# Batch 1's centred rows turned by transposing DMAs, with the start of the order made anew

## The chip, the cores and the metric

The kernel runs on one core of a Trainium2 chip. The metric is the device time of one execution in microseconds (us); the median of several runs is compared. TensorE (PE) multiplies matrices, VectorE (DVE), ScalarE (ACT) and GpSimd (POOL) work element by element, SyncE (SP) issues most DMAs. Each engine works through its own queue in order, and the queues wait for each other by semaphores.

## The reference, cut to what matters

```python
# x: 8 x 8 x 512 x 64, state: 8 x 8 x 32 x 64 (batch, head, rows, 64), float32
a  = softmax(scale * x @ state^T, over the 32 state rows);  xread = a @ state      # 512 rows
a2 = softmax(scale * state @ x^T, over the 512 rows of x);  sread = a2 @ x         # 32 rows
x2 = concatenate([xread, sread], rows), heads laid side by side                    # 8 x 544 x 512
X = np.fft.fft(x2, axis=1)
X = np.fft.fft(X, axis=2)
u = x2 + np.real(X)
un = (u - mean(u)) / sqrt(var(u) + 1e-6)                                           # per row
out = u + np.maximum(un @ w_ch1, 0.0) @ w_ch2                                      # 512 -> 2048 -> 512
```

## The kernel before

The batches run one after the other, and each goes through four parts:

- `attend(b)`: the rows `xin` (the bfloat16 copy of the loaded `xs`) and the state `stb` are turned into `xT` and `sT`; products `esp` give the scores, exponentials on ScalarE give `E`, `EE` and `ET`; the products `xrp`, `xfp` and `srp` read with them, and the result is scaled into `XR` and `XF`, rows in reverse and in forward order.
- `transform(b)`: the two-dimensional Fourier transform as products with tables of sines and cosines: `gp` over the columns (copied to `G`), `yp` over the rows. `U` is the sum of a block of rows with its transform; a row's mean and variance are `mv`. `centre` writes the centred rows `ub` (bfloat16), and `turn_u` turns a block of 128 x 512 of them into columns of `unT`. There are four blocks for each batch.
- `layer1(b)`: products `ph` of `unT` with `w1`, and a relu on ScalarE into `hT`.
- `layer2(b)`: products `po` of `hT` with `w2`, scaled by `rstd` and added to `U` on VectorE (`ot`). From batch 2 on this is a form with fewer products (`poA`, `poB`).

`turn_x`, `turn_state` and `turn_u` have two forms. In one, four TensorE transposes write a PSUM tile (`xTp`, `sTp`, `tp`) and a copy takes it to SBUF. In the other, one transposing DMA on SP's queue does the same from SBUF to SBUF. Which is used is set by batch: `x_by_dma, u_by_dma = 2, 2` means that the DMA is used from batch 2 on for both.

Nothing is issued where it is written. A `Recorder` keeps every engine call as a numbered group, and `play` issues the groups in the order of the list `ORDER`, so that each engine's queue is that list restricted to its own groups. Every instruction therefore has the line of the recorder's helper (L63), and the profile is read by tile names. `BANKS` says in the same way which of six PSUM banks each product tile uses, and which buffer an output tile uses. In the first 70 us the layers of batch 0 are interleaved with the attention and the transform of batch 1 and with the attention of batch 2.

Some names of that stretch: `warm` products only keep TensorE busy while data is loading; a `gate` operation reads one or a few elements of a tile so that what stands behind it on its engine, or what reads the gate, comes after that tile; the weights come as eight DMAs on POOL's queue, four for `w1` and four for `w2`; `load_state(1, 2)` loads the state of batch 1 on SP's queue. ScalarE's sine (for the tables `TS`, `TC`) and exponential need different tables, and each change between them is an ACT_TABLE_LOAD; an activation on `gate2` asks for the sine's ahead of the tables:

```python
    nc.scalar.activation(gate2[:, 1:2], gate2[:, 0:1], AF.Sin)
    state_ones(0, 2)
    state_blocks(0, 1)
    cast_x(0, nc.scalar.copy, 2, 3)
```

Of the kernel before, what the change touches and what calls it, by code (L numbers as in the profile page):

```python
# [49 lines left out]
class _Engine:  # L50
# [3 lines left out]
    def __getattr__(self, what):  # L54
# [14 lines left out]
        19 62 66 61 9-10 12 1 7 11 2 5 4 3 163 8 49 13 6 298 14 55 15 17 16 50 22 0 75-82 29 143 25 27 26 47 28 38 31 41 23  # L69
        144-145 40 39 32 146-147 30 20 46 21 42 48 148 43-45 149 18 24 34-35 33 37 36 72-74 83-118 130 119 329 120-121 123 122  # L70
        155 131 157 124 156 168 330 172 125 141 170 126 169 171 173 142 176 127-129 133-134 184 178 180 192 68 54 159 69-71 177
        185 193 59-60 58 67 64 316 63 65 187 189 186 135-137 188 138 194 196 195 197 139-140 153-154 216 174 331-332 175 206-210
        212 179 211 181 221 219 213 222 132 150-151 182 152 190 198-199 191 217 214 218 200 263 160 167 201-202 51 265 161
        203-204 267-268 165-166 205 299 162 56 261-262 300 158 264 304 266 297 307 303 302 301 57 228 232 229 220 225-227 224
        233 245 223 244 241 183 215 236-240 252-254 231 235 234 230 276-277 247-248 278-279 246 250-251 259 257 255 269 256 272
        249 242-243 258 271 274 284 270 273 317 312 310 309 319 315 314 313 311 318 280-283 285 290 292-293 291 294 275 286 288
        323 322 287 327 326 320 289 321 328 343 324 341 325 345 339 347 340 348 355 333 337 353 378 351 335 386 354 352 346 387
        361 360 342 338 344 385 379 362-365 367 308 260 366 368 52 296 358 382 381 398 356 390-391 380 383-384 521 392-393 396
        394 439 401 400 399 336 357 359 397 334 402-404 406 405 408 407 409 522 413-414 505 523-524 410 415 412 411 441 525 305
        371 370 369 373 422 374 419 375 426 424 420 423 53 526 421 417-418 459 457 349 376 455 453 461 476 465 388 463 473 469  # L80
        467 460 395 350 440 462 456 454 377 458 464 470 468 466 389 472 488 474 480 518 451 481 445-446 449 482 450 487 484 491
        442 492 447 485 496 475 477-478 443 448 495 500-501 506 429-430 428 427 452 591 493 486 479 483 529 536 497 516 498 489
        517 502 499 490 578 164 306 579 507 503 574 527 504 471 508 372 576 580 528 575 416 577 433 432 435 437 434 431 436 543
        582 512 532 519 530 494 583 514 444 520 531 550 533 539 537 589 509 540 538 560-563 510 555 544 556 545 511 438 546 549
        772 547 553 548 559 552 557 554 584 558 598 592 534 585-586 630 622 600 564 569 567 601 606 614 587-588 593 602-603 573
        568 572 570-571 607-608 596 595 597 594 609-610 621 611 613 612 616-617 625 618 627 626 620 619 604 541 624 632 637 599
        535 551 631 615 605 590 623 638 542 652 677 633 641 639 635 565 634 642 640 636 646 661 668 628 566 653 662 678 647 649
        671 654 648 655 670 663 669 664 684 689 685 690 680 682 650 644 659 672 629 683 658 681 667 651 688 693 645 673 660
        714-715 751 704 736-737 757 761 716-717 701 656 700 740 699 295 698 718 728 727 729 657 730 733 732 731 581 674-675
        694-695 679 767 762 782 708 774-775 768 922 745 744 705 771 742 769 741 746 743 738 752 739 754 756 706 763-764 758 755  # L90
        753 776-777 709 778 783 779-780 791 786 790 794-795 787 789 788 702-703 676 713 796 697 765 818 812 864 784 792 802 797
        804 816 814 871 759 808 719 820 766 813 865 819 793 803 785 798 815 805 817 760 809 821 830 823 711 725 720 710 825 726
        712 707 722 806 810 873 799 828 734 880 837 723 721 826 824 827 735 800 781 801 747-748 849 862 842 831 872 807 874 829
        881 836 835 846 850 838 840 839 841 811 863 845 843 852 870 724 773 770 851 750 844 866 858 856 875 911 832 893 877 884
        882 892 833 883 876 857 696 853 859 867 887-888 919 904 886 902 907 974 908 889-890 912 903 921 665-666 891 822 896 691
        847 895 848 899 898 897 900-901 692 686 643 687 954 932 914 878 909-910 920 894 955 928-929 934 968 834 960 957 959 925
        923-924 879 1102 941-942 970 980 996 963 917 976 905 1035 991 987 939 969 975 997 1046 981 933 906 1036 964 918 992 940
        930 913 931 935 943 916 915 937 944-948 938 971 965 949 966 986 950 977 988 967 953 952 951 978 984 993 1103 927 936 958
        973 926 962 961 956 1047 989 982 1007 985 994 979 990 983 1008 1048 1003 998 1012 1040 1009 1053 1022 1024 1058 1101
        1000 999 1001 1014 1005 1013 1004 1002 1041 1006 1054 1010 1025 1011 1060 1086 1061 1051 1067 1077-1078 1049 1062  # L100
        1015-1016 1063 1023 1059 1018 1027 1052 1064 1070 868 1071 1073-1074 1072 860 869 861 854 1075-1076 855 1079-1080 1050
        1087 1140 1017 1026 1031 1042 1280 1105 1104 1107 515 1134 1139 1137-1138 1106 1082 1037 1097-1098 1055 1119 1146 1084
        1236 1112 1069 1065 1056 1083 1099-1100 1066 1088 1038 1091 1113 1132 1108 1148 1094 1213 1166 1164 1110 1120 1019 1028
        1147 1237 1133 1114 1089-1090 1115-1116 1118 1117 1126 1122 1095 1081 1121 1124 1123 1141 1096 1143 1142 1130 1125 1111
        1144 1158 1205 1154 1092 1193 1162 1168 1127 1160 1149 1032 1085 1214 1165 1043 1109 1159 1167 1155 1206 1093 1194 1169
        1145 1131 1128 1161 1163 1174 1231 1207 1188 1219 1150 1175-1177 1151 1178 1057 1039 1136 1135 513 1179 1232 1220
        1181-1182 1180 1279 995 1020-1021 425 1029 1238-1239 1183 1172 1225 1156 1264 1191 1229 1226 1157 1192 1230 1185 1208
        1173 1171 1186 1189 1240 1184 1241 1190 1187 1243 1201 1196 1224 1197 1281-1282 1129 1068 1153 1200 1285 1195 1283-1284
        1209 1215 1255 1245 1256 1260 1227 1288 1257-1258 1244 1228 1247 1274 1261 1198 1030 1242 1044 1248 1250 1254 1249 1170
        1253 1199 1045 1033-1034 1275-1276 1221 1233 1335 1272 1277 1222 1289 1259 1265 1304 1273 1278 1308 1268 1305 1270  # L110
        1290-1291 1315 1252 1251 1267 1316 1292 1266 1234 1286 1321 1331 1297 1364 1343 1319 1327 1337 1376 1310 1407 1262 1293
        1269 1294 1296 1306 1295 1322 1312 1314 1332 1344 1299 1313 1300 1303 1301 1309 1342 1361 1302 1271 1202 1210 1287 1336
        1298 1320 1328 1216 1377 1365 1395 1408 1311 1338 1333 1325 1339 1359 1329 1340 1334 1326 1330 1317 1354 1402 1390 1360
        1318 1391 1403 1263 1398 1378 1435 1409-1410 1345 1357 1356 1355 1358 1379 1411 1399 1412 1348 1346-1347 1349 1367 1372
        1352 1368 1353 1307 1323 1235 1223 1386 1380 1366 1371 1413 1419 1421 1211-1212 1420 1217 1424-1425 1203-1204 1218 1341
        1423 1422 1369-1370 1392 1404 1426-1427 1416 1400 1362 1446-1447 1396 1384 1350 1428 1436 1429 1440 1393 1405 1363 1373
        1397 1351 1385 1401 1454-1455 1481 1491 1431 1441 1474 1461 1536 1450 1492 1482 1475 1462 1451 1439 1438 1418 1448-1449
        1456-1457 1468 1437 1458 1460 1459 1463 1476 1478 1464 1414-1415 1432 1445 1465-1466 1452 1512 1570 1499 1501 1489 1443
        1453 1477 1467 1444 1430 1497 1493 1469 1479 1537 1442 1513 1500 1490 1502 1498 1494 1472 1470 1473 1480 1516 1483 1507
        1495 1485 1524 1563 1519 1517-1518 1496 1520 1486 1508 1510 1509 1504 1511 1394 1406 1521 1505 1433 1538 1484 1527 1381  # L120
        1532 1525 1514 1564 1387 1528 1434 1515 1506 1523 1539 1522 1544 1554 1567 1558 1556 1550 1557 1540 1546 1471 1526 1531
# [50 lines left out]
def kernel(  # L172
# [8 lines left out]
    nc = Recorder(tc.nc)  # L181
# [304 lines left out]
    def stats_of(u, name, roots=None):  # L486
# [12 lines left out]
        else:  # L499
            roots.append(root)  # L500
        return mv, rstd

    first_roots = []


    x_by_dma, u_by_dma = 2, 2


    turned = {}

    def attend(b):
        g4, bq = b // 4, b % 4
# [1042 lines left out]
```

## Time and profile before

| | |
|---|---|
| runs | 288.75, 287.68, 288.82 us; median 288.75 |
| profiled execution | 287.47 us, of which the span of the profile is 285.7 us |
| granted TensorE clock | 0.997 |
| busy: TensorE, VectorE, ScalarE, GpSimd | 275.2 (96%), 210.6 (74%), 162.0 (57%), 92.5 us (32%) |
| ACT_TABLE_LOAD | 4, of 1.28 us each, at 1.90, 6.32, 11.58 and 19.53 us |
| first layer-1 product of batch 0, of batch 1 | 22.39 us, 54.00 us |
| copies `unT<-tp` on ScalarE | 6 in batches 0 and 1, 565 to 587 ns each |
| transposing DMAs `unT<-ub` on SP | 26, from 75.0 us on |

A row of the timeline has the start and the duration in us, the engine, the operation with its output and inputs, and how many instructions the row holds; in brackets stands how long the engine was idle before it, and what ended that. Matmuls overlap, so the pace of TensorE is read from one start to the next, not from the duration of one. Times are from the start of the span.

### The profile page before, as it was taken

To read this page: it belongs to the slowest core of one execution; us is meant where nothing else is said; L and a number is where in the kernel's file an instruction comes from. 1 tells how busy PE (TensorE), PEld (TensorE's weight loads), DVE (VectorE), ACT (ScalarE), POOL (GpSimd) and SP (SyncE) were. 2 spreads that over 40 slices of the span, in tenths; PEclk is the share of its full clock that TensorE was granted. 3 is DMA by queue.
4 is the path that set the end of the run, shared out by engine and by line. 5 is a ranking of instruction groups with operands and counts; after the bars stand their busy time and mean duration, and the time that the engine had idled before them with its cause. 6 is when DMAs were issued, how large, how long until landed. Compare 5 with 4: busy or idle time off the path is not lost.

```text
span 285.7 us, 6835 instructions
## 1 busy us (share of the span) xinstructions
PE 275.2 (96%) x2615; PEld 199.0 (70%) x2644; DVE 210.6 (74%) x554; ACT 162.0 (57%) x327; POOL 92.5 (32%) x227
## 2 busy tenths in 40 slices
PE   7899999999999999999999999999999999999993
PEld 6788985555655778567758777576577667686882
DVE  6877777468899988985798688959766578224892
ACT  7897656746936576368377564586566653254000
POOL 8392476670660033502712119006200028000000
PEclk9999999999999999999999999999999999999998
DMA  8999959966366346861379640413201520978366
GB/s 156 185 181 190 202 95 181 197 146 153 83 157 103 93 116 156 107 170 25 80 169 194 149 94 19 98 53 65 84 0 48 151 65 18 182 149 136 92 162 184
DMA packets 110972, 34.91 MB, mean 122 GB/s; under 512 B 101996, under 2 KB 106476, under 8 KB 110940
## 3 DMA queue, kind: packets, MB, share of 16 engines
q1 hardware_dynamic: 100220, 28.72, 47.5%
q0 software_dynamic: 4224, 4.19, 9.7%
q10 hardware_dynamic: 6496, 1.57, 2.6%
q8 instruction: 20, 0.33, 0.5%
q14 instruction: 12, 0.10, 0.1%
HBM read 22.41 MB, written 14.02 MB: 128 GB/s over the span
## 4 chain that ended last, share of the span: by engine, by line
PE 87%; DVE 7%; DMA 2%; issue 1%; ACT 1%; SPq 1%; DVEq 0%
PE ph L63 39%; PE poA L63 18%; PE poB L63 13%; PE gp L63 4%; PE po L63 3%; PE yp L63 2%; DVE U L63 2%; DMA xs<-in_x_dram 2%; PE esp L63 2%; PE eTp L63 1%; PE xrp L63 1%; DVE XR L63 1%; PE xfp L63 1%; DVE ot L63 1%; SPq L63 1%
## 5 line engine op out<-in xcount | busy, mean ns | idle before, releaser
L63 PE MATMUL ph<-unT,w 128*128 128x512 bf16 (+2 forms) x743 | 127.9, 315 | 1.4
L63 ACT ACTIVATE hT<-ph 128x512 bf16<-128x512 f32 x128 | 72.1, 596 | 76.6 <-PE ph L63 76.3
L63 PEld LDWEIGHTS <-w 128*128 128x128 bf16 x768 | 64.3, 98 | 42.5 <-issue 0.6
L63 PEld LDWEIGHTS <-hT 128*128 128x128 bf16 x632 | 60.4, 98 | 14.8 <-issue 0.3
L63 DVE SCALAR_TENSOR_TENSOR ot<-poA,rstd,U 128x256 f32<-128x256 f32 (+1 forms) x46 | 21.7, 475 | 16.5 <-PE poA L63 13.8
L63 POOL CAST xin<-xs 128x2048 bf16<-128x2048 f32 (+3 forms) x14 | 14.5, 1046 | 48.5 <-PE poA L63 20.3
L63 PE MATMUL poB<-w,hT 128*128 128x256 bf16 x224 | 28.2, 273 | 0.0
L63 POOL TENSOR_TENSOR rstd<-rstd,mhalf 128x1 f32<-128x1 f32 x34 | 20.3, 604 | 1.1
L63 POOL TENSOR_TENSOR rstd<-mv,epst 128x1 f32<-128x1 f32 x14 | 2.8, 211 | 42.9 <-DVE mv L63 42.9
L63 ACT CAST G<-gp 128x288 bf16<-128x288 f32 (+2 forms) x31 | 12.8, 477 | 5.6 <-PE gp L63 5.3
L63 ACT ACTIVATE ub<-U,S 128x512 bf16<-128x512 f32 (+1 forms) x22 | 15.1, 706 | 1.5 <-DVE U L63 1.3
L63 PE MATMUL po<-w,hT 128*128 128x512 bf16 x60 | 15.4, 379 | 0.2
L63 PE MATMUL poB<-TA,SA 128*128 128x256 bf16 x120 | 15.5, 273 | 0.1
L63 PE MATMUL poA<-TA,SB 128*128 128x256 bf16 x120 | 15.6, 273 | 0.0
L63 DVE SCALAR_TENSOR_TENSOR U<-yp,XF 128x2 f32<-128x2 f32 (+1 forms) x24 | 10.0, 419 | 7.5 <-PE yp L63 5.3
L63 DVE SCALAR_TENSOR_TENSOR ot<-poB,rstd,ot 128x256 f32<-128x256 f32 x30 | 14.2, 478 | 1.0 <-PE poB L63 0.8
L63 PE MATMUL poA<-TC,hT 128*128 128x256 bf16 (+1 forms) x120 | 14.5, 265 | 0.1
L63 POOL COPY XT<-XR 32x514 bf16<-32x514 bf16 x7 | 4.2, 605 | 31.8 <-DVE U L63 15.8
L63 PE MATMUL poA<-w,hT 128*128 128x256 bf16 x112 | 14.5, 273 | 0.0
L63 ACT ACTIVATE junk<-U,S 128x512 bf16<-128x512 f32 x20 | 14.3, 716 | 0.2
L63 PE MATMUL poA<-TB,hT 128*128 128x256 bf16 x112 | 14.3, 273 | 0.0
L63 DVE SCALAR_TENSOR_TENSOR ot<-poB,rstd,U 128x256 f32<-128x256 f32 x15 | 7.2, 478 | 9.0 <-PE poB L63 9.0
(197 smaller groups left out, 478.3 us busy)
## 6 DMA issues: line engine op xcount, KB each, us to landing
xs<-in_x_dram SPq DMA_DIRECT2D x22, 256.0 KB, 3.8
w<-in_moe_w_ch_dram POOLq DMA_DIRECT2D x8, 512.0 KB, 6.8
out_dram<-ot SPq DMA_DIRECT2D x15, 256.0 KB, 2.4
r_dram<-ot SPq DMA_DIRECT2D x14, 256.0 KB, 2.4
out_dram<-r_dram SPq DMA_DIRECT2D x14, 256.0 KB, 3.7
xs<-in_x_dram SPq DMA_DIRECT2D x8, 192.0 KB, 4.9
xs<-in_x_dram ACTq DMA_DIRECT2D x2, 256.0 KB, 4.7
l_dram<-ot SPq DMA_DIRECT2D x2, 256.0 KB, 2.0
```

The source lines that it names most:

```text
L63: self._rec.add(self._name, lambda: f(*args, **kw), key)
```

## The change

`u_by_dma` goes from 2 to 1. Batch 1's four `turn_u1` calls each become one transposing DMA on SP's queue instead of four TensorE transposes and one copy on ScalarE, and the recorder has 1744 groups instead of 1748. The order is made anew for the part in which batches 0 and 1 are worked on; the last 568 groups are the same (their numbers 4 lower). The strings in `BANKS` are made anew as well. TensorE's own order is the same as before from about 70 us on. Batch 1's state load, twelfth on SP before, follows straight behind batch 0's loads.

```diff
 ORDER = [i for p in """
-        19 62 66 61 9-10 12 1 7 11 2 5 4 3 163 8 49 13 6 298 14 55 15 17 16 50 22 0 75-82 29 143 25 27 26 47 28 38 31 41 23
-        144-145 40 39 32 146-147 30 20 46 21 42 48 148 43-45 149 18 24 34-35 33 37 36 72-74 83-118 130 119 329 120-121 123 122
...
+        19 58 4 11-12 10 298 9 7 1 14 2 8 13 6 16 3 17 15 55 54 5 50 22 21 25 0 38 20 143 23 29-30 144 26 145-146 27 147 40 39
+        41 28 42-43 46 44 148 31 149 32 150 45 75-82 18 34 24 37 72 36 33 35 83-109 130 110-123 131 155 157 124 156 168 172 125
...
-    x_by_dma, u_by_dma = 2, 2
+    x_by_dma, u_by_dma = 2, 1
...
-    turn_u1(0, 1, nc.scalar.copy)
+    turn_u1(0, 1)
...
-    turn_u1(0, 0, nc.scalar.copy)
+    turn_u1(0, 0)
...
-    turn_u1(1, 1, nc.scalar.copy)
+    turn_u1(1, 1)
...
-    turn_u1(1, 0, nc.scalar.copy)
+    turn_u1(1, 0)
```

What the new order moves on each engine's queue, by name:

- ScalarE: the first cast `stb<-gen` of batch 0's state stands ahead of the `gate2` activation; it was behind it.
- SP: batch 1's state load, as told; a piece of `load_x(3)` and the pieces of `load_x(2)` stand ahead of batch 2's `xT` transposes and of batch 1's `unT` transposes. That piece of x(3) waits for the POOL operation `gate<-xs,w1`.
- POOL: that operation, and the DMA of the first quarter of `w2`, stand behind the copy `XT<-XR` of batch 1, which waits for VectorE's `XR`; the first quarter of `w2` was issued at 21.38 us before. The casts of batch 1's rows stand earlier.
- TensorE: seven groups of batch 0's `po` stand ahead of batch 1's first layer-1 product.
- VectorE: `U` and `ub` of batch 0's block (0, 0) stand later.

## The prediction

> **What bounds the kernel now.** I read the page first: busy shares, then the chain that ended last.
>
> ```profile
> PE 275.2 (96%) x2615; PEld 199.0 (70%) x2644; DVE 210.6 (74%) x554; ACT 162.0 (57%) x327; POOL 92.5 (32%) x227
> ...
> PE 87%; DVE 7%; DMA 2%; issue 1%; ACT 1%; SPq 1%; DVEq 0%
> ```
>
> TensorE is busy 96% of 285.7 us and carries 87% of the chain. So the change is worth what it takes out of TensorE's own stream, in issue time or in stalls. Next the waits of TensorE, to see which stalls there are to win.
>
> ```profile
> PE warm L63 <- DVE blank L63: 1.5, 1, 1.5
> PE xTp L63 <- DVE xin L63: 1.4, 3, 0.9
> PE tp L63 <- DVE U L63: 0.4, 1, 0.4
> PE xfp L63 <- DVE XR L63: 0.2, 1, 0.2
> PE xTp L63 <- POOL xin L63: 0.2, 1, 0.2
> PE xfp L63 <- DVE XF L63: 0.2, 1, 0.2
> ```
>
> Columns: who waited for whom, us in total, times, longest. All of it lies in batches 0 and 1; nothing is left to win later. Then TensorE's timeline around batch 1's turns (start, us, operation, count).
>
> ```profile
> 49.45 0.61 PE L63 MATMUL tp<-ident,ub 128*128 128x128 bf16 x8
> 50.45 0.38 PE L63 MATMUL tp<-ident,ub 128*128 128x128 bf16 x4 [0.39 <-DVE U L63]
> ...
> 52.68 0.38 PE L63 MATMUL tp<-ident,ub 128*128 128x128 bf16 x4
> ...
> 54.00 1.03 PE L63 MATMUL ph<-unT,w 128*128 128x512 bf16 x4
> ```
>
> Sixteen transposes; eight take 0.61 and four 0.38, so one more costs 0.23/4 = 0.057 us of issue. The eight are issued by 49.45 + 8 x 0.057 = 49.91 and the next starts at 50.45: a stall of 0.54. Batch 1's first layer-1 product starts at 54.00.
>
> **The change, part by part.** I worked against the profiled execution: span 285.70, its time 287.47, which is 1.28 under the median of 288.75. Nothing under 0.5% of that (1.44 us) can be told from no change.
>
> *Removed from TensorE.* 16 x 0.057 = -0.91 us, all on the path.
>
> *Stalls that go with it.* The 0.54 at 50.45 goes, since the instruction that waited is gone. Two more lie in the part whose order is made anew: two xTp transposes start at 19.89 and are issued by 20.00, the next waits for POOL's cast until 20.35 (0.35); sixteen ph start at 27.14, are issued by 28.05, and the xfp behind them starts at 28.40 (0.35). In the new order batch 1's casts stand earlier on POOL, so I count the first as gone and half the second (bounds: none, both whole). Sum -0.54 - 0.35 - 0.18 = -1.07.
>
> *Removed from ScalarE.* Four copies unT<-tp, 0.565 to 0.587 us each, 2.3 us. ScalarE is 57% busy and none of TensorE's waits names it: nothing. What hides it is TensorE's queue; without that cover the gain would be at most these copies.
>
> *Added on SP.* Four DMA transposes. The 26 of later batches take 1.19 to 2.43 us of SP's time each and land 2.3 (median) to 3.6 us after issue. What counts is when they are issued, and SP works in order. Ahead of them now stand a piece of x(3) that waits for a POOL operation (a small add that reads w1 and xs), the pieces of x(2), batch 3's state, four xT transposes. Carrying before's durations along the new orders, POOL gets to that add at about 37, the xT transposes run at 42.3 to 47.3 (in before from 43.86), and the four unT transposes are issued at about 48.0, 49.35, 50.6 and 51.85. ub is there by 47.7, 49.3, 50.4 and 51.1. The last lands at 51.85 + 2.3 = 54.15, at slowest 55.4. Seven products of layer 2 are moved ahead, so TensorE gets to batch 1's layer 1 at 54.7. I take 0; bounds 0 and +0.7, and from there every us that SP is later is one that TensorE stands.
>
> *Moved on POOL.* The DMA of the first quarter of w2 stood at 21.38; in the new order POOL first waits for XR of batch 1 (about 29.0) and does folds, so by rows it is issued at about 32.7. This is how long such a load takes (DMAs of w: minimum, median, maximum):
>
> ```profile
> DMA to landing us min/median/max: 5.4/6.8/9.1
> ```
>
> It lands at 38.1, 39.5 or 41.8; TensorE needs it for batch 0's first layer-2 product at about 39.0. By the median 0.5 late. I take 0 here, as layer 1 in front of it is also later by the start below; bounds 0 and +2.8.
>
> *Moved on ScalarE, at the start.* This is what the words of the change do not say. ScalarE's timeline of before:
>
> ```profile
> 1.90 1.28 ACT L63 ACT_TABLE_LOAD   x1 [1.90 <-issue]
> 3.20 0.20 ACT L63 ACTIVATE gate<-gate 128x1 f32<-128x1 f32 x1
> 3.41 0.91 ACT L63 CAST stb<-gen 32x128 bf16<-32x128 f32 x3
> 4.42 0.62 ACT L63 CAST xin<-xs 128x512 bf16<-128x512 f32 x1
> ...
> 6.32 1.28 ACT L63 ACT_TABLE_LOAD   x1
> ...
> 9.81 1.75 ACT L63 ACTIVATE EE<-esp 128x512 bf16<-128x512 f32 x3 [0.48 <-PE esp L63]
> 11.58 1.28 ACT L63 ACT_TABLE_LOAD   x1
> ```
>
> The gate activation loads the sine table first, while the state is still coming. In the new order a cast of the state stands before that gate. The program then has five table loads instead of four: a default one for the cast, then the sine one, and the first can start only when the state has landed, at 3.00 instead of 1.90. In before's durations: load to 4.33, cast, load to 5.94, cast of x at 6.16 (was 4.42), exponent table to 9.92, copy of xT to 10.7, last of the EE exponentials at 12.7 (was 11.56): +1.1. Part is hidden, since the last quarter of x lands at 8.34 and VectorE's chain behind has slack: Sm at about 16.1 (was 15.48), first ph at about 22.95 (was 22.39). I take +0.55; bounds 0 (all hidden) and +2.4 (1.28 for the load, 1.10 for the later start).
>
> The Trainium skill ("ScalarE: Activation LUTs", What ACT_TABLE_LOAD costs) speaks against this order more strongly: it gives about 1.28 us for a load and as much again, 1.38, for a drain, 2.66 for each switch of tables. This trace shows the load at 1.28 and the next activation 0.02 us behind it (1.90 + 1.28, then 3.20), so no drain; by the page the bound would be +3.8 instead of +2.4.
>
> *New small waits.* eTp and tp near 25.5 wait for exponentials and a ub that stand later on ScalarE and VectorE, yp waits for copies of G: by rows +0.4 and +0.2, some of it in time that the later start has already given. I take +0.30; bounds 0 and +0.6.
>
> *State of batch 1 sooner.* One SP issue of 0.5 moved from 9.24 to behind batch 0's loads. Batch 0's loads are not moved; batch 1's x is pushed by 0.5 and needed only near 19: nothing. If that cover is gone, 0.5.
>
> *Later on.* From about 70 us TensorE's order is the same as before and there are no stalls, so nothing is given back; the offset stays to the end.
>
> Sum: -0.91 - 1.07 + 0.55 + 0.30 = -1.13. Profiled 286.34; with the 1.28, **287.6**: 0.4% faster, inside what can be told from no change.
>
> **The rivals.**
>
> *A: the start costs nothing* (because TensorE and VectorE wait for the x landing at 8.34 there, as 1.4 us of waits for xin show), and both removed stalls go whole. Then -0.91 - 1.24 = -2.15: 286.6, faster. Against it: the EE exponentials stand on the way to XR, and 12.7 is past what the landing hides.
>
> *B: POOL's queue decides; slower.* w2's first quarter and SP's piece of x(3) both stand behind POOL's wait for XR of batch 1. The time is over before's by 1.44 only if the stall is 2.57 or more: w2 landing at 41.6, that is a load of 8.9 us from 32.7 or a median one from 34.8, with POOL 2 us later than I worked out. Such a delay moves unT too, by 1.5 past the slack. Priced at +3.3: -1.13 + 3.3 gives 290.9. For it: POOL's spans are the least sure, and the slack is under 1 us. Against it: the loads in the middle of the kernel have a half empty DMA (5 to 9 tenths).
>
> *C: the start at its full price.* -0.91 - 1.07 + 0.30 + 2.4 = +0.7: 289.5, no change. TensorE then also idles longer at 5 to 7 us, which could lower its clock; before shows a granted clock of 9 tenths through that slice, with 0.9 us the longest wait.
>
> *D: the change does not do what it says to the time.* The transposes fill waits that reappear elsewhere: 0, 288.75.
>
> **How the numbers follow.** Forecast 0.40, A 0.27, B 0.18, C 0.10, D 0.05. About a quarter of the forecast's own band (287.0 to 288.3) lies under 287.31, so faster is 0.27 + 0.10 = 0.37; slower is most of B and a third of C, 0.20; the rest, 0.43, is no change. The likeliest case's own range is 287.0 to 288.3. Signs are mixed, so the whole range reaches from A with a little more (286.2) to B (290.9).
>
> **What would show it.** Five ACT_TABLE_LOADs, the first at 3.0, and the last EE exponential near 12.7: the start. First ph near 22.95. No wait of tp at 50, unT<-ub transposes on SP at 48 to 52, landing before TensorE's first ph of batch 1 at 54.7. No wait of po on DMA w near 39. The gp of batch 2 (69.00 in before) about 1.1 earlier, with everything behind it at the same offset. I am wrong if TensorE waits for w or unT there, if the offset grows or shrinks after 70 us, or if TensorE's granted clock falls in the first 10 us.

## The result and the profile after

The changed kernel takes 295.34 us (293.08 to 296.48, 6 runs), the kernel before beside it 288.32 (287.56 to 289.13, 6 runs): a ratio of 1.0244, interval 1.0217 to 1.0272. It is slower by 7.0 us, where 0.4% faster was forecast, and outside the range. The profiled execution took 295.62, its span is 293.8: 8.1 us longer than before's 285.7.

The page of the changed kernel, busy shares, TensorE's granted clock in 40 slices, and the chain that ended last:

```profile
PE 277.2 (94%) x2599; PEld 199.8 (68%) x2628; DVE 215.0 (73%) x554; ACT 161.6 (55%) x324; POOL 93.1 (32%) x227
...
PEclk9799999979999999999999999999999999999998
...
PE 85%; DVE 6%; ACT 3%; DMA 2%; issue 1%; SPq 0%; ACTq 0%; DVEq 0%
```

The sixteen transposes are gone (2615 to 2599 matmuls), and yet TensorE is busy for 2.0 us longer; its clock fell twice, the two 7s. VectorE, which lost nothing, is busy for 4.4 us more. TensorE's waits say where:

```profile
PE ph L63 <- DMA unT<-ub: 3.7, 1, 3.7
PE xTp L63 <- ACT xin L63: 2.0, 1, 2.0
PE gp L63 <- DVE SS L63: 1.7, 1, 1.7
PE warm L63 <- DVE blank L63: 1.7, 1, 1.7
PE gp L63 <- DVE XQ L63: 0.5, 1, 0.5
```

The waits on ScalarE's xin, on SS and XQ and the one on unT are new; those on tp and on VectorE's and GpSimd's xin went. There is none on `w`. Three starts on TensorE give the time by stage:

| kernel | first ph of batch 0 | first gp of batch 2 | last matmul |
|---|---|---|---|
| before | 22.39 | 69.00 | 280.76 |
| changed | 25.73 (+3.34) | 77.19 (+8.19) | 288.87 (+8.11) |

So 3.3 us are lost by 26 us, 4.9 more by 77 us, and nothing changes after. **The start**, on ScalarE:

```profile
3.50 1.28 ACT L63 ACT_TABLE_LOAD   x1 [3.50 <-DMA gen<-in_state_dram]
4.80 0.30 ACT L63 CAST stb<-gen 32x128 bf16<-32x128 f32 x1
5.11 1.28 ACT L63 ACT_TABLE_LOAD   x1
6.41 0.20 ACT L63 ACTIVATE gate<-gate 128x1 f32<-128x1 f32 x1
6.52 0.60 ACT L63 CAST xin<-xs 128x512 bf16<-128x512 f32 x1
```

The extra table load is there, behind the state, which landed at 3.50 in this execution. TensorE has no rows until 7.17. What comes next is on VectorE, first in the changed kernel, then in the one before; GpSimd's row of the changed kernel stands last:

```profile
18.12 2.19 DVE L63 TENSOR_TENSOR SS<-Sm 128x256 bf16<-128x256 bf16 x2
```

```profile
16.21 0.50 DVE L63 TENSOR_TENSOR SS<-Sm 128x256 bf16<-128x256 bf16 x2
```

```profile
18.35 1.81 POOL L63 CAST xin<-xs 128x512 bf16<-128x512 f32 x3
```

The same two sums take 2.19 us instead of 0.50 while GpSimd casts beside them (1.57 and 0.69 each, 0.29 before). **The wait for unT**, on SP, on GpSimd and on TensorE:

```profile
23.76 18.17 SPq L63 DMA_DIRECT2D xs<-in_x_dram  x8
...
47.80 6.54 SPq L63 DMA_TRANSPOSE xT<-xin  x4
54.39 0.59 SPq L63 DMA_DIRECT2D xs<-in_x_dram  x1
55.09 6.05 SPq L63 DMA_TRANSPOSE unT<-ub  x4
```

```profile
39.83 0.20 POOL L63 TENSOR_TENSOR gate<-xs,w 128x4 f32<-128x4 f32 x1
...
47.56 0.75 POOL L63 CAST xin<-xs 128x16 bf16<-128x16 f32 x2 [5.04 <-DMA xs<-in_x_dram]
```

```profile
62.41 0.88 PE L63 MATMUL ph<-unT,w 128*128 128x512 bf16 x2 [3.72 <-DMA unT<-ub]
...
64.16 2.80 PE L63 MATMUL ph<-unT,w 128*128 128x512 bf16 x8
...
67.02 1.89 PE L63 MATMUL ph<-unT,w 128*128 128x512 bf16 x8
```

SP's piece of x(3) waits for GpSimd's add (done at 40.0); the last pieces of x(2) behind it are issued only at 40.8 and 41.3, and GpSimd waits for them until 47.56; the xT transposes wait for that cast, and the unT transposes for those on SP, though their ub were ready at 51.2, 52.8, 53.9 and 54.7. TensorE stands for 3.72 us, and then eight ph take 2.80 instead of 1.89: the granted clock is 0.67 between 64 and 67 us.

### The profile page after: what moved, and what is told of

Its sections match the earlier page's. It is cut to its first block, busy times and chain, and to the rows that moved or that the text cites. A ratio compares the mean times of both kernels' runs of the same rounds, so it can differ in the third digit from the quotient of the medians.

```text
span 293.8 us, 6814 instructions
## 1 busy us (share of the span) xinstructions
PE 277.2 (94%) x2599; PEld 199.8 (68%) x2628; DVE 215.0 (73%) x554; ACT 161.6 (55%) x324; POOL 93.1 (32%) x227
## 3 DMA queue, kind: packets, MB, share of 16 engines
q10 hardware_dynamic: 6496, 1.57, 2.5%
## 4 chain that ended last, share of the span: by engine, by line
PE 85%; DVE 6%; ACT 3%; DMA 2%; issue 1%; SPq 0%; ACTq 0%; DVEq 0%
PE ph L63 37%; PE poA L63 17%; PE poB L63 13%; PE po L63 4%; PE gp L63 4%; PE yp L63 3%; PE esp L63 2%; PE warm L63 1%; DVE SS L63 1%; PE xrp L63 1%; PE eTp L63 1%; DVE ot L63 1%; PE xfp L63 1%; DMA gen<-in_state_dram 1%; ACT L63 1%
## 5 line engine op out<-in xcount | busy, mean ns | idle before, releaser
L63 POOL CAST xin<-xs 128x2048 bf16<-128x2048 f32 (+3 forms) x14 | 15.4, 1122 | 58.9 <-DMA xs<-in_x_dram 46.9
L63 PE MATMUL po<-w,hT 128*128 128x512 bf16 x61 | 14.8, 379 | 0.1
```

The source lines that it names most:

```text
L63: self._rec.add(self._name, lambda: f(*args, **kw), key)
```

## The experiments

The theory after this reading: two costs that are apart, the start (the table load, with what follows it) and SP's order (x(3)'s piece ahead of x(2)'s last ones). The rivals: the late start alone causes both; or transposing DMAs are too slow for this place whatever the order. Orders are told by the group numbers of `ORDER`.

**gate_first.** On the changed kernel:

```diff
-  18 34 24 37 72
+  18 24 34 37 72
```

> The changed kernel, with one move on ScalarE: the sine's gate activation ahead of the first cast of batch 0's state, as before the change. Theory: in the changed kernel the start costs 3.3 us at the first ph (25.73 against 22.39), all of it through this: two table loads behind the state's landing at 3.50, then 2.0 us in which TensorE idles, its pace back from 56 to 107 ns, and VectorE's SS beside GpSimd's casts (1570 ns instead of 294). With the gate first, four table loads, the first at 1.9, xin cast near 4.5, first ph at 22.4 to 23.2, SS back under 420 ns. The wait for unT near 58.7 stays, 3 to 4 us, since SP's chain moves with the start: about 292.3 us. Rival (one cause): the late start is why unT is late too; then both go and the time is about 288.5. Rival (the table load is hidden): nothing moves, 295.

293.03 us; ratio to before 1.0169 (1.0147 to 1.0191). First ph at 23.67, TensorE's wait for SS 0.9, for unT 2.6 us:

```profile
59.21 1.02 PE L63 MATMUL ph<-unT,w 128*128 128x512 bf16 x3 [2.58 <-DMA unT<-ub]
```

The wait for unT stays, so the late start is not the one cause. But only 2.1 of the 3.3 us at the start come back: SS still takes 581 and 694 ns, beside casts that now start at 16.9.

**x3_later.** On the changed kernel:

```diff
-  312-313 437 314-315 319 318 435
+  312-313 314-315 319 318 435 437
```

> The changed kernel, with one move on SP: the piece of x(3) that waits for GpSimd's add behind the last pieces of x(2), batch 3's state and sT instead of ahead of them. Theory: the last small pieces of x(2) are then issued at about 31 instead of 40.8, are there when GpSimd comes to their casts (about 42.5 instead of 47.56), the four xT transposes run at 42.7 to 49 instead of 47.8 to 54.35, and the unT transposes are issued as their ub comes (51.3 to 54.9), landing by 57.2. TensorE comes to batch 1's layer 1 at 58.7: the wait of 3.7 us goes, and the slow pace behind it: about 289.8 us. The start is as in the changed kernel, first ph at 25.7. Rival (the four transposes are too slow by themselves, 6 us of SP): the wait stays above 2 us, 293 to 295. Rival (it is only the late start): nothing moves.

291.81 us; 1.0131 (1.0107 to 1.0156). SP's timeline:

```profile
41.70 6.35 SPq L63 DMA_TRANSPOSE xT<-xin  x4
...
50.76 5.39 SPq L63 DMA_TRANSPOSE unT<-ub  x4
```

The xT transposes are 6.1 us sooner, the unT transposes wait only for their ub, and TensorE does not wait for unT any more. One position on SP's queue was worth 3.5 us of the 7, of which a part may be the start's: in this trace the state landed at 2.93 instead of 3.50, TensorE waited 1.2 us for xin without a fall of its clock, and the first ph is at 24.74, 1.0 sooner, though nothing at the start was moved. The gain is not the 5.5 expected: the waits for XQ grew from 0.5 to 1.7 us, and that for SS stayed at 1.7.

**both.** The two moves together.

> Both moves of the two runs before together. Theory: the two costs are apart and add up, 3.0 to 3.3 for the start and 5.4 to 5.8 for the wait with the slow pace behind it: 286.5 to 287.0 us, 0.5% under the kernel before, close to what was predicted for the change. Rival (they share a cause): no better than the better of the two, 288.5 to 290.

289.92 us; 1.0064 (1.0040 to 1.0087). The moves gain 2.3 and 3.5 us one by one and 5.4 together, so they are nearly apart. But the result is 2.1 us over the kernel before, not 1 under it: a third cost is left. Its trace has first ph at 23.70 (+1.31), and waits on VectorE's SS (0.9) and XQ (0.9 at 42 us, and one like it at 71).

**dma_only.** The kernel before with the four DMA turns, and nothing else:

```diff
-    x_by_dma, u_by_dma = 2, 2
+    x_by_dma, u_by_dma = 2, 1
...
-    turn_u1(0, 1, nc.scalar.copy)
+    turn_u1(0, 1)
```

> The kernel before, its order kept, with only the four turns of batch 1 as transposing DMAs, at the places of TensorE's transposes, the fourth behind its ub. Theory: TensorE comes to batch 1's first ph at 54.00 - 0.91 - 0.54 = 52.55; the fourth ub is there at 52.2, its DMA is issued at about 52.8 and lands at 55.1, so TensorE waits 2.6 us and may fall to the slow pace behind it (up to 1.3 more): 289.5 to 291. Rival (the transposes are hidden): 287.0. Rival (transposing DMAs are slow whatever their place): a wait of 4 us or more, 291 or more.

291.50 us; 1.0116 (1.0090 to 1.0143): the transposes alone, in an order that was not made for them, cost 3.6 us. TensorE's timeline:

```profile
55.81 1.65 PE L63 MATMUL ph<-unT,w 128*128 128x512 bf16 x4 [2.17 <-DMA unT<-ub]
```

The four are issued at 49.41, 50.72, 52.02 and 53.33, one each 1.3 us; the last ub is done at 52.45, and TensorE starts on its columns at 55.81, 3.4 us later. With TensorE and a copy it was 1.5 us (52.16 to 53.69 in before). The granted clock then is 0.66 from 55 to 60 us.

**w_first and gate_ss**, on `both`: GpSimd's casts of batch 1's x later, to part them from SS. In w_first w1's last DMA goes ahead of the casts; in gate_ss also the one-element copy gate<-SS, so that no cast runs until SS is done.

```diff
-  261-262 264 205 ... 253-254 ... 260        (both)
+  205 261-262 264 ... 253-254 ... 260        (w_first)
+  205 ... 253-254 260 261-262 264            (gate_ss)
```

> The kernel with both moves, and on GpSimd the issue of w1's last quarter (0.75 us) ahead of the three casts of batch 1's x instead of behind them. Theory: VectorE's sums SS<-Sm, which read two inputs from SBUF, are held while GpSimd casts (581, 694 and 836 ns beside the casts of 16.9 to 18.7, against 294, 288 and 419 in the kernel before, where the casts start at 18.2). With the casts from about 17.7 on, the first two SS take about 290 each and are done by 17.1, TensorE's wait for SS of 0.9 us goes, first ph at 22.4 to 22.8 instead of 23.6: about 289.0 us, 0.9 less than with both moves. Rival (SS is late because of the softmax in front of it): SS still ends near 17.7 and the wait stays.

> The kernel with both moves, and on GpSimd the casts of batch 1's x held until VectorE's SS is done: the one-element copy gate<-SS, which stood near 33 us, goes in front of them, and w1's last quarter and nothing else in front of that. Theory (GpSimd's casts hold VectorE's SS): in w_first the casts only met the later SS, 1018 and 827 ns; now no cast runs before the last SS, so all four are at 288 to 420, SS done by 17.5, TensorE's waits for SS and NN near 17 and 19 (1.1 us in all) gone, first ph at 22.4 to 22.8, about 289.0 us. The casts run at 17.7 to 19.6, in time for xTp at 21.6. Rival (issuing w1's DMAs on GpSimd holds VectorE as much): SS at 16.2 to 17 still takes 600 to 700, first ph stays above 23.2.

w_first: 290.34 us, 1.0073 (1.0048 to 1.0099), no gain: the first SS still takes 703 ns and the later ones, now beside the casts, 1018 and 827. gate_ss: 290.39 us, 1.0079 (1.0057 to 1.0101). In its trace VectorE is as in the kernel before, and TensorE's wait for SS is gone; but TensorE now waits for the casts themselves:

```profile
16.30 0.50 DVE L63 TENSOR_TENSOR SS<-Sm 128x256 bf16<-128x256 bf16 x2
```

```profile
21.00 0.23 PE L63 MATMUL xTp<-ident,xin 128*128 128x128 bf16 x1 [0.32 <-POOL xin L63]
21.65 0.57 PE L63 MATMUL xTp<-ident,xin 128*128 128x128 bf16 x7 [0.41 <-POOL xin L63]
```

The casts start at 19.78 instead of 17.7, as casts of stb that wait for a landing at 18.3 come before them: that step of the expectation was wrong. So GpSimd's casts do hold VectorE's sums, and issuing w1's DMAs on GpSimd did not in this run (they stand beside SS in gate_ss as well, and it takes 293 and 286 ns). But parting the two costs as much as it gains. Why the first SS of w_first takes 703 ns, with only such an issue beside it, stays open.

**casts_act**, on `both`: the five casts of x(2) on ScalarE, and in `ORDER` moved to where it was idle.

```diff
-        nc.gpsimd.tensor_copy(xin_bufs[0][:, i, 1 + lo:1 + hi], ...
+        nc.scalar.copy(xin_bufs[0][:, i, 1 + lo:1 + hi], ...
```

> The kernel with both moves, and the five casts of x(2) on ScalarE instead of GpSimd, two where ScalarE is idle at 35 and three at 39.3. Theory: in the middle, too, GpSimd's casts hold VectorE's two-input operations of batch 1: SS 1376 ns for 696, XO 976 for 659, XE 1232 and 574 for 685 and 169, 1.9 us in all, and TensorE waits 1.1 for XQ at 42 because of it. On ScalarE the casts do not hold them: SS, XO and XE at 650 to 700 ns, no wait for XQ at 42, about 288.8 us. Rival (XQ is late because VectorE has other work in front of it, BNStats above all): the durations fall but the wait stays over 0.7 us. Rival: relu on ScalarE becomes late and TensorE waits for hT or a bank instead, 290 or more.

> A second look at casts_act, whose times scatter from 289.1 to 293.1 where its profiled run was at 289.2. If the scatter is TensorE's wait for unT (batch 1's layer 1 is reached 1.1 us sooner there, while the fourth unT lands when its ub lets it), a slower run shows PE ph <- DMA unT<-ub of 1 to 3 us near 56; if it is the start, the wait is for xin before 8 us.

290.87 us (289.12 to 293.11, 10 runs), 1.0090 (1.0057 to 1.0124). Of VectorE's long ones of batch 1, the first SS went from 1376 to 880 ns (the second from 661 to 850), XO from 976 to 690, XE from 1232 to 780, and the wait for XQ at 42 is gone in both traces: first ph of batch 1 at 55.89 in the first, for 56.99 in `both`. The time did not fall. The second trace, of an execution at 291.47, has waits of 0.55 us for unT, 0.4 for xT and 0.8 for XQ from 56 to 72 us; the first has only one of 0.6 for XQ there. So in the slower execution the gain is lost again at transfers that come late. Why the times scatter is not settled by two traces.

**all**: both moves, gate_ss and casts_act together.

> Everything that the theory names put right in the changed kernel: the sine's gate first, x(3)'s piece later on SP, the casts of batch 1's x behind SS, the casts of x(2) on ScalarE. Theory: 289.9 with both moves, less 1.0 for SS, less 1.0 for XQ at 42: 287.9 us, and where nothing else is late as little as 287.0, level with the kernel before or a little under it. Rival (the casts on ScalarE made the times of casts_act scatter by 4 us, so something there is late in some runs): 289 to 291 with the same scatter.

289.68 us (288.59 to 291.22); 1.0059 (1.0036 to 1.0082). Not under the kernel before, as the rival said. Its waits are for xin on POOL (1.3), xT by DMA (0.7), XQ (0.6) and unT (0.5).

**gate_late.** The kernel before, with only the table load of the change:

```diff
-  24 34
+  34 24
```

> The kernel before, with one move on ScalarE: the first cast of batch 0's state ahead of the sine's gate activation. No other part of the change is in it. It prices the extra table load by itself: by the prediction's step first ph 0.55 later (22.95) and 288.4 us; by what the changed kernel showed, a first load only at 2.9 to 3.5, the cast of x at 6.2 to 6.5, TensorE idle for 2 us and back at the slow pace, first ph 1.5 to 2.2 later: 289.4 to 290.1. Rival (the load is hidden by the landing of x): no difference.

288.66 us; 1.0020 (0.9998 to 1.0042), 0.6 us over before, if anything. In its trace the first load is at 3.05, and TensorE waits for the cast:

```profile
7.33 0.40 PE L63 MATMUL xTp<-ident,xin 128*128 128x128 bf16 x4 [1.24 <-ACT xin L63]
```

First ph at 23.26, +0.87. TensorE is idle for 1.24 us here and keeps its pace of 56 ns; in the changed kernel it was idle for 2.03 and fell back to 107 ns from 8.1 to 11.4 us.

**dma_filled.** dma_only, with a product of layer 2 and the ten eTp ahead of batch 1's first ph.

```diff
-  493 ... 546 ... 535 533 507
+  493 ... 507 ... 535 533 546
```

> The kernel before with the four DMA turns of batch 1, and TensorE's order changed in one place: a product of layer 2 (0.86 us) and the ten eTp (0.5) go ahead of batch 1's first ph, to fill the wait. Theory: with the DMA turns alone TensorE waits 2.2 us for the fourth unT, which lands 3.3 us after its ub is done, as SP issues one transpose each 1.3 us; 1.36 us of work in front leaves a wait of 0.8 to 1.0, too short to lose the pace: 289.4 us or a little less, 2 below the DMA turns alone. Rival (something else than the fourth landing holds ph): the wait stays at 2 us, 291.5.

291.75 us; 1.0117 (1.0058 to 1.0176). The wait for unT fell from 2.2 to 0.9, as expected, but a wait of 2.0 us of a ph on VectorE's XR appeared at 67.28 and the slow pace behind it. By its name this is a PSUM bank that is freed later; that it is one was not tried.

**two_dma.** The kernel before with only the two earliest turns by DMA, and the third turn, for which TensorE waited 0.54, behind one more product.

```diff
-            if b >= u_by_dma:
+            if b >= u_by_dma or b == 1 and (k, r) in ((1, 1), (0, 0)):
...
-  489 ... 490 ... 580
+  580 489 490
```

> The kernel before with only the two turns of batch 1 by DMA whose ub is ready when SP is free (blocks (1, 1) and (0, 0), ub done at 48.3 and 48.9), the other two left to TensorE, and the turn that made TensorE wait 0.54 us at 50.45 put behind one more product of layer 2. Nothing else of the change. Theory: the two DMAs are issued at 49.2 and 50.4 and land by 53.0, TensorE comes to batch 1's first ph at 54.00 - 8 x 0.057 - 0.54 = 53.0, so the saving is kept: 1.0 us off, 287.0 where before is at 288.0, a ratio of 0.996 to 0.998. Rival (a transposing DMA also delays what stands behind it on SP, the pieces of x(3), by 2.5 us): the pieces are needed only near 56.8 by GpSimd's cast, and if that is late, TensorE's layer of batch 2 gets it back: no gain, 288.0.

289.32 us; 1.0045 (1.0033 to 1.0057): slower. Batch 1's first ph is 0.5 us sooner (53.48 for 54.00), half of what the theory had. What it got wrong stands later, on GpSimd and TensorE:

```profile
59.95 1.89 POOL L63 CAST xin<-xs 128x2048 bf16<-128x2048 f32 x1 [4.58 <-DMA xs<-in_x_dram]
```

```profile
68.22 0.29 PE L63 MATMUL esp<-sT,xT 128*128 128x64 bf16 x4 [0.55 <-DMA xT<-xin]
...
83.45 0.40 PE L63 MATMUL xrp<-stb,ET 128*128 128x260 bf16 x2 [1.25 <-DVE XF L63]
```

The two transposes push x(3)'s pieces on SP back by 2.4 us; the cast that was at 56.76 is at 59.95, xT comes too late for esp at 68, and XF for xrp at 83. The rival had the mechanism; the price is higher than its "no gain", 1.4 us over the kernel before.

The new order with batch 1's turns left on TensorE was not run, so how much of the 7.0 us the order costs without the transposes is not shown.

## Why the prediction was wrong

- **Transposes removed, 0.91 us**: they are gone, but no version that puts them on SP kept the gain.
- **Stalls removed, 1.07, and new small waits, 0.30**: the three stalls did go. But the term of new waits named only eTp, tp and yp; TensorE's wait for VectorE's SS measured 1.7 us, and that for XQ 0.5 (1.7 in `both`), so these terms together lost instead of gaining. This is a failed step that no rival held: I carried before's durations along the new orders, and VectorE's do not stay the same when GpSimd's casts come to lie beside them.
- **The start, 0.55**: by itself the table load was sized rightly within the noise (gate_late: 0.6 in the time, 0.87 at the first ph). In the changed kernel it met a later landing of the state (3.50 for 3.00), the fall of the clock, which C had named without a price, and SS, and the first ph was 3.34 late (2.35 in x3_later, which has the same start). gate_first gives 2.3 us of time back.
- **The unT transposes, 0, with 0.7 as the upper bound**: 3.72 us of wait, and an estimated 1.6 to 1.8 behind it at the slow pace. The failed step is SP's chain. I had GpSimd's add at 37, and it ended at 40.0, with the start late. From there to the xT transposes I had 5.3 us, and it took 7.8: x(2)'s last pieces, which stand behind the piece that waits, were issued at 41.3 and used at 47.56, and I gave their landing no time of its own. The xT and unT transposes then took 2.6 us more than before's durations gave. The last columns landed at 62.28 instead of 54.15, 8.1 us late, and TensorE came for them at 58.69, only 4.0 late. x3_later, where the wait is gone, shows that the position of x(3)'s piece is the cause.
- **w2's first quarter, 0**: right, and for the reason given, though by a start much later than I had it: issue (35.25), landing (41.29) and the first product that needs it (42.18) were 2.6, 1.8 and 3.2 us later than forecast, so that the 0.5 late became 0.9 early. The DMA engines that I called half empty were busy 5 to 9 tenths by my own row.
- **Rival B** had the mechanism (GpSimd's queue holds SP's piece), but its price rested on w2, and a wait for unT of 1.5 us, where it was 3.72 with a slow clock behind it. C and B came true together, and the range let in only one of them at a time; even their prices added give 292.8 us, 2.6 under the result.
- **Later on, nothing given back**: right for the changed kernel (+8.19 at 77 us, +8.11 at the end). Not all waits of before lie in batches 0 and 1, though: the one of 0.15 us for XF stands at 79.92, in batch 2.

The gate and x(3)'s piece are 5.4 us of the 7.0. `both` is still 2.1 over the kernel before, which was at 287.85 beside it and not at 288.32. Its waits are on VectorE beside GpSimd's casts and on late transfers, but taking such waits away (gate_ss, casts_act, all) did not bring the time down. So what these 2.1 us consist of is not shown; the cost of the transposes on SP (3.6 alone in dma_only) may be part of them.

The Trainium skill ("SBUF — State Buffer", SBUF: two separate sides) states that a VectorE operation with two SBUF inputs and a GpSimd operation that reads SBUF exclude each other for a whole instruction. The rows agree that the casts hold the sums (1570 ns for 294; 293 again in gate_ss with the casts away), but by the profile's starts the one held here had started first, at 18.12 against 18.35, where the page gives the ports to the one that starts first.

The skill ("TensorE: Matmul & The Clock Gate", Part 1) puts the fall to the slow clock at an idle window of about 3.4 us. Here it fell after waits of 2.03, 2.17 and, in dma_filled, 1.99 us as well as 3.72, and held after 1.24 and, in gate_first, after 2.58.

## What to carry to other kernels

A turn moved from TensorE to a DMA queue costs that queue's time: price what stands behind it (here loads for a batch two further on), its latency from the last input (3.4 us against 1.5), and what holds the queue ahead of it, with the landing of every transfer in that chain. When an order is made anew, list which VectorE operations with two inputs come to lie beside GpSimd's casts; durations of the old order do not hold there. And where several terms sit with less than a microsecond of slack, let the range hold them late together.

## What the runs showed of the hardware that was not expected

- Two sums on VectorE took 1570 and 694 ns instead of 294 and 288 beside GpSimd's casts, and were back at 293 and 286 when the casts were elsewhere; issues of DMAs on GpSimd beside them did no harm in that run, while in w_first the first sum took 703 ns with no cast beside it.
- TensorE's pace halved after idle times of 2.0 to 2.2 us in three kernels (granted clock 0.90 over the first 10 us in the changed kernel, 0.66 from 55 to 60 us in dma_only, 0.76 from 65 to 72 us in dma_filled) and stayed after 2.58 us in gate_first.
- The last small piece of x(2) was used 6.3 us after its issue (41.27 to 47.56), where the median quarter of x lands in 4.1. The four quarters of w2, issued at 35.3 to 40.0, were under way then and took 6.0 to 12.1 us; that they delayed the piece was not tried.
